# First MoE of a fused retention and MoE kernel: relu and square emitted right behind the first product, rounding ahead of the chunks' copies, the stream's second product in another bank

## The chip, the cores and the metric

The kernel runs on one core of one Trainium2 chip. The metric is the device time of one execution in microseconds (us). Lower is better. Besides the plain timed runs there is one execution under the hardware profiler, from which all rows below come.

## The reference

Three stages follow each other: a retention (linear attention with decay) over 4 batches, 8 heads, 768 positions and 64 features; a dense MoE over all 3072 tokens; and a second MoE with 8 experts, to which tokens are assigned greedily by their logits. The change is in the dense one.

```python
def _moe_ref(x, w_in, w_out, s, b):      # x 3072x512, w_in 512x2048, w_out 2048x512
    h = x @ w_in
    r = np.maximum(h, 0.0)
    g = s * (r * r) + b
    return (g @ w_out).astype(np.float32)

def _moe2_ref(x, w_gate, w1, w2):
    logits = x @ w_gate                  # then: greedy, 384 tokens for each of 8 experts
    for e in range(E):
        mask = assigned == e
        out[mask] = np.maximum(x[mask] @ w1[e], 0.0) @ w2[e]
```

## The kernel before

Matrices are fed to TensorE as two rounded parts, a high one and a low one (`xh` and `xl`, `h` and `l` of a weight, `rh` and `rl` of the squared activations), and a product is three matmuls: high by high, high by low, low by high. So each activation of the dense MoE has to be rounded (high part) and subtracted (low part) before it can be used.

The 3072 tokens are 24 chunks of 128. Chunks 0 to 5 go through a first stage, whose order of work a planner writes out. Chunks 6 to 19 go through **the stream**, the function `moe1`, with which the change deals. It has five blocks: four of three chunks and one of two. For each block it walks over the 16 slices of 128 of the 2048 hidden features. One step n is one block and one slice, 80 steps in all. Step n has two units of work:

- `hu(n)`: first `low_parts` of the step before (VectorE makes `rl` of step n-1, L466), then **the first product** (`h_unit`, L445): 12 matmuls of 384 columns (256 in the last block) into bank 3 of PSUM, always bank 3.
- `xu(n)`: **the second product** (`x_unit`, L477) of step n-2: nine matmuls of 512 columns (six in the last block) that are added to banks 0, 1 and 2, one bank a chunk. If this was the last slice of its block, the finished chunks are then copied out of their banks (`x_out`, L485, ScalarE). Then ScalarE works on step n: relu from bank 3 into the buffer `r` (L589, there is only one such buffer, `WR`), square in place (L458), and the rounding copy into `rh` (L459). `rh` and `rl` have two slots, by n modulo 2, so the rounding of step n overwrites what the second product of step n-2 reads.

So TensorE's order is: first product of n, second product of n-2, first product of n+1, second product of n-1, and so on. The first product of n+1 writes bank 3 and must wait until the relu of n has read it.

Between the units stand side streams (`Weave`): `attn`, which does the retention of the next chunks in steps (scale q on VectorE, L247; scores on TensorE, L352; mask, L357; values, state and cross products, L365, L373, L379; then ScalarE copies the chunk's result `xh`, L421 or L418, and the state `sbd`, L385, and VectorE makes `xl`, L422), and `logits_gen`, which lets VectorE multiply finished rows with the gate's columns (L497). A side step is due at a time counted along the stream, and is emitted ahead of the unit that is next when it comes due, so it may stand ahead of `hu(n)` or between `hu(n)` and `xu(n)`.

When the stream starts, the first stage has one second product of two chunks left (`REST`). It is emitted right behind `hu(0)`, with the copies of its two chunks. At steps 0 and 1 there is no second product yet, so the first products of steps 1 and 2 stand next to each other on TensorE.

After the stream come the last four chunks (`h_pair`), the search for the assignment, and the second MoE. Every engine works through its own instructions in the order in which they are emitted.

Of the kernel before, what the change touches and what calls it, by code (L numbers as in the profile page):

```python
# [27 lines left out]
AF = mybir.ActivationFunctionType  # L28
# [116 lines left out]
def kernel(  # L145
# [29 lines left out]
    NF = w64.shape[0]  # L175
# [16 lines left out]
    PE, ACT, DVE, POOL, SP = nc.tensor, nc.scalar, nc.vector, nc.gpsimd, nc.sync  # L192

    def bank(i):
        return psum.tile([128, 512], F32, name=f"b{i}", tag=f"b{i}")
# [23 lines left out]
    WR = work.tile([128, 2 * TB], F32, name="r")  # L219
# [219 lines left out]
    def h_part(f, ph, x, kcs):  # L439
        xh, xl = x  # L440
        wh, wl = WT[2 * f]
        for kc in kcs:
            ks = slice(kc * 128, (kc + 1) * 128)
            for n, (a, b) in enumerate(((wh, xh), (wh, xl), (wl, xh))):
                PE.matmul(ph, a[:, ks], b[..., kc, :], start=(kc == 0 and n == 0), stop=(kc == KC - 1 and n == 2))  # L445

    def h_unit(x, f, hb, n):

        ph = bank(hb)[:, 0:n]
        h_part(f, ph, x, range(KC))  # L450
        return ph
# [3 lines left out]
    def r_split(r, rh, rl):  # L455


        ACT.activation(r, r, AF.Square)  # L458
        ACT.activation(rh, r, AF.Copy)  # L459
        LOW.append((r, rh, rl))  # L460
        return rh, rl

    def low_parts():
        while LOW:
            r, rh, rl = LOW.pop(0)
            DVE.tensor_tensor(rl, r, rh.bitcast(F32), op=OP.subtract)  # L466

    def x_unit(chs, f, xb, r):

        rh, rl = r  # L470
        wh, wl = WT[2 * f + 1]
        for t, ch in enumerate(chs):
            if f == 0:
                X2[ch] = bank(xb[t])
            ts = slice(t * C, (t + 1) * C)
            for i, (a, b) in enumerate(((rh, wh), (rh, wl), (rl, wh))):
                PE.matmul(X2[ch], a[:, ts], b, start=(f == 0 and i == 0), stop=(f == NF - 1 and i == 2))  # L477
# [5 lines left out]
    def x_out(ch):  # L483
        U[ch] = tmp.tile([128, Dm], F32, name="tmp")
        ACT.activation(U[ch], X2[ch], AF.Copy, scale=sb[:, 0:1])  # L485
# [70 lines left out]
    def moe1(blocks, before):  # L556


        seq = [(i, f) for i in range(len(blocks)) for f in range(NF)]
        units, R = [], {}  # L560
        for n in range(len(seq) + 2):
            if n < len(seq):
                i, f = seq[n]
                chs = blocks[i]
                x = XS[(chs[0] - CPB) // 3 % 2] if len(chs) == 3 else [t[:, chs[0] // 2 % 2] for t in XP]

                def hu(n=n, i=i, f=f, x=x, w=len(chs) * C):
                    if f == 0:
                        before(i)
                    low_parts()  # L570
                    R[n] = h_unit(x, f, 3, w)
                units.append((len(chs) * 700, hu))

            def xu(n=n):
                if n == len(seq):
                    low_parts()
                    before(len(blocks))
                if n > 1:
                    i, f = seq[n - 2]
                    x_unit(blocks[i], f, range(3), R.pop(n - 2))  # L580
                    if f == NF - 1:
                        for ch in blocks[i]:
                            x_out(ch)
                if n < len(seq):

                    w = len(blocks[seq[n][0]]) * C
                    ws = slice(n % 2 * T3, n % 2 * T3 + w)
                    ph = R[n]
                    ACT.activation(WR[:, 0:w], ph, AF.Relu)  # L589
                    R[n] = r_split(WR[:, 0:w], RH[:, ws], RL[:, ws])  # L590
            units.append((len(blocks[seq[n - 2][0]]) * 695 if n > 1 else 0, xu))
        return units

# [213 lines left out]
    blocks = [range(ch, ch + 3) for ch in range(CPB, NC - 6, 3)] + [range(NC - 6, NC - 4)]  # L807
    nxt = []

    def before(i):  # L810

        while nxt and not nxt[0].done:
            nxt[0].step()
        if i < len(blocks):
            last = i + 1 == len(blocks)
            nxt[:] = [Side(attn(range(NC - 4, NC), (2800, 2500)) if last else attn(blocks[i + 1]),
                           wv.t + 6000 * (i == 0))]
            wv.add(nxt[0])
        else:
            split_last()  # L820

    for u in moe1(blocks, before):
        wv.unit(*u)
        if REST:
            wv.unit(1395, REST.pop())
            x_out(CPB - 2)
            x_out(CPB - 1)
# [52 lines left out]
    def h_pair(f):  # L880
        ph = bank(2 + f % 2)
        for i in range(2):
            wv.unit(1300, lambda: h_part(f, ph, XP, range(2 * i, 2 * i + 2)))
        r = r2[:, f % 2]
        ACT.activation(r, ph, AF.Relu)

        R4[f] = WT[2 * f]
        r_split(r, *R4[f])
        low_parts()

# [39 lines left out]
    for f in range(NF + 1):  # L930
        if f < NF:
            h_pair(f)
        if f == 1:
            wv.until(lambda: len(CONST) > NF)
            X2["l"] = bank(7)
        if f == NF:
            fill(4)
        if f >= 1:
            wv.unit(440, lambda: l_unit(f - 1))
# [642 lines left out]
```

## Time and profile before

| | |
|---|---|
| median of 3 runs | 995.09 us (994.17 to 997.15) |
| the profiled execution's own time | 993.34 us |
| span of its instructions | 991.6 us |
| TensorE busy | 965.8 us (97% of the span) |
| VectorE busy | 696.6 us (70%) |
| ScalarE busy | 445.5 us (45%) |
| mean granted TensorE clock | 0.993 |

The span runs from the first to the last instruction in the trace; the execution's own time is 1.7 us longer than it. Busy time counts an engine as busy while at least one of its instructions runs. The stream takes the stretch from about 181 to 557 us.

### The profile page before, as it was taken

The numbers are of one execution on the slowest core, as the hardware profiler recorded it, in microseconds if no ns is written. First come the engines' busy times: TensorE is split into PE (matmuls) and PEld (weight loads), VectorE is DVE, ScalarE is ACT, GpSimd is POOL, SyncE is SP. The second block draws the span as 40 slices with busy tenths as digits, with TensorE's granted clock in tenths as the row PEclk, the third lists the DMA queues.
The fourth block names the chain that finished last, engine by engine and source line by source line (L and its number), as shares of the span: only waits on it lengthen the run. The fifth ranks groups of instructions, "written<-read, shape, count | busy, mean of one in ns | idle before, by whom it ended". The sixth has DMA issues, their size and how long they took to land.

```text
span 991.6 us, 17302 instructions
## 1 busy us (share of the span) xinstructions
PE 965.8 (97%) x6721; PEld 837.0 (84%) x6721; DVE 696.6 (70%) x1677; ACT 445.5 (45%) x818; POOL 91.4 (9%) x153
## 2 busy tenths in 40 slices
PE   7899999999999999999999999999999999999997
PEld 6788888788888888888988877888888888888996
DVE  5899993687888977988465342578888877886310
ACT  6666665433343333343343454155455363455211
POOL 2000000000000000000000100032213042140111
PEclk8999999999999999999999999999999999999999
DMA  9234342422132022122023100063454373365100
GB/s 348 93 130 164 131 151 94 171 75 82 46 84 98 12 64 76 46 72 65 1 76 117 55 1 1 13 223 119 143 165 141 117 232 113 124 215 200 54 32 32
DMA packets 32946, 103.49 MB, mean 104 GB/s; under 512 B 4512, under 2 KB 4896, under 8 KB 32864
## 3 DMA queue, kind: packets, MB, share of 16 engines
q1 hardware_dynamic: 28080, 88.15, 27.0%
q0 software_dynamic: 3920, 12.89, 3.8%
q10 hardware_dynamic: 864, 1.35, 0.4%
q8 instruction: 52, 0.85, 0.3%
q14 instruction: 30, 0.25, 0.1%
HBM read 89.53 MB, written 12.85 MB: 103 GB/s over the span
## 4 chain that ended last, share of the span: by engine, by line
PE 88%; issue 4%; DMA 4%; ACT 2%; POOL 1%; DVE 1%; SPq 0%; POOLq 0%; ACTq 0%; DVEq 0%
PE b L445 27%; PE b L477 22%; PE b L1401 11%; PE b L1381 10%; PE b L910 5%; PE b L1060 3%; PE b L365 3%; PE b L352 3%; PE b L379 2%; DMA eraw<-in_w_dram 1%; PE b L1256 1%; PE b L373 1%; PE b L893 1%; POOL out_dram L1409 1%; DMA first1h<-in_qkv_dram 1%
## 5 line engine op out<-in xcount | busy, mean ns | idle before, releaser
L497 DVE SCALAR_TENSOR_TENSOR scr<-tmp,wg 128x512 bf16<-128x512 f32 x288 | 198.4, 689 | 8.4 <-ACT tmp L485 2.0
L477 PE MATMUL b<-h,rh 128*128 128x512 f32 x320 | 127.0, 397 | 0.6 <-ACT rh L741 0.6
L477 PE MATMUL b<-l,rh 128*128 128x512 f32 x320 | 125.9, 393 | 0.0
L477 PE MATMUL b<-h,rl 128*128 128x512 f32 x320 | 125.8, 393 | 0.0
L445 PE MATMUL b<-xh,h 128*128 128x512 f32 (+2 forms) x320 | 113.4, 355 | 4.8 <-ACT r L589 4.7
L445 PE MATMUL b<-xh,l 128*128 128x512 f32 (+2 forms) x320 | 111.2, 348 | 0.0
L445 PE MATMUL b<-xl,h 128*128 128x512 f32 (+2 forms) x320 | 111.2, 347 | 0.0
L1381 PE MATMUL b<-gh,h 128*128 128x384 f32 x256 | 89.7, 350 | 0.0
L1353 ACT ACTIVATE h<-eraw 128x1024 fp32r<-128x1024 f32 x64 | 67.2, 1057 | 42.6 <-DMA eraw<-in_w_dram 39.1
L1381 PE MATMUL b<-gh,l 128*128 128x384 f32 x256 | 86.2, 337 | 0.0
L1381 PE MATMUL b<-gl,h 128*128 128x384 f32 x256 | 86.0, 336 | 0.0
L589 ACT ACTIVATE r<-b 128x384 f32<-128x384 f32 (+1 forms) x80 | 37.6, 469 | 106.1 <-PE b L445 87.1
L1363 DVE TENSOR_TENSOR l<-eraw,h 128x1024 fp32r<-128x1024 f32 x64 | 77.9, 1227 | 8.8 <-ACT h L1353 8.4
L1389 DVE SCALAR_TENSOR_TENSOR hl<-b,hh 128x384 fp32r<-128x384 f32 x64 | 35.5, 555 | 61.5 <-ACT hh L1386 61.0
L1401 PE MATMUL b<-h,hh 128*128 128x512 f32 x192 | 78.0, 406 | 0.0
L1386 ACT ACTIVATE hh<-b 128x384 fp32r<-128x384 f32 x64 | 31.4, 490 | 103.0 <-PE b L1381 95.5
L1401 PE MATMUL b<-h,hl 128*128 128x512 f32 x192 | 75.6, 394 | 0.0
L1401 PE MATMUL b<-l,hh 128*128 128x512 f32 x192 | 75.4, 393 | 0.0
L445 PEld LDWEIGHTS b<-xh,h 128*128 128x128 f32 x320 | 60.5, 189 | 16.3 <-ACT r L589 8.3
L466 DVE TENSOR_TENSOR rl<-r,rh 128x384 fp32r<-128x384 f32 (+1 forms) x80 | 42.2, 528 | 44.8 <-ACT rh L459 44.5
L477 PEld LDWEIGHTS b<-h,rl 128*128 128x128 f32 x320 | 60.1, 188 | 13.5 <-DVE rl L743 0.4
L477 PEld LDWEIGHTS b<-h,rh 128*128 128x128 f32 x320 | 60.2, 188 | 12.0 <-ACT rh L741 0.8
(274 smaller groups left out, 1993.2 us busy)
## 6 DMA issues: line engine op xcount, KB each, us to landing
eraw<-in_w_dram SPq DMA_DIRECT2D x64, 512.0 KB, 4.3
q<-in_qkv_dram SPq DMA_DIRECT2D x36, 512.0 KB, 5.1
raw<-in_w_dram SPq DMA_DIRECT2D x32, 512.0 KB, 4.4
x2d<-tmp SPq DMA_DIRECT2D x21, 256.0 KB, 6.0
qdec<-in_dec_dram SPq DMA_DIRECT2D x17, 256.0 KB, 2.7
wg<-in_wgT_dram SPq DMA_DIRECT2D x4, 512.0 KB, 4.2
x2d<-tmp ACTq DMA_DIRECT2D x3, 256.0 KB, 2.3
first1h<-in_qkv_dram SPq DMA_DIRECT2D x1, 512.0 KB, 7.1
```

The source lines that it names most:

```text
L445: PE.matmul(ph, a[:, ks], b[..., kc, :], start=(kc == 0 and n == 0), stop=(kc == KC - 1 and n == 2))
L466: DVE.tensor_tensor(rl, r, rh.bitcast(F32), op=OP.subtract)
L477: PE.matmul(X2[ch], a[:, ts], b, start=(f == 0 and i == 0), stop=(f == NF - 1 and i == 2))
L497: DVE.scalar_tensor_tensor(scr, x, 1.0, WG[e], op0=OP.mult, op1=OP.mult, accum_out=of[:, e:e + 1])
L589: ACT.activation(WR[:, 0:w], ph, AF.Relu)
L910: PE.matmul(XB[c][:, ns], a[:, cs], b[:, ns], start=(f == 0 and i == 0), stop=(f == NF - 1 and i == 2), skip_group_check=True)
L1353: ACT.activation(hi, ERAW[n], AF.Copy)
L1363: DVE.tensor_tensor(lo, ERAW.pop(n), hi.bitcast(F32), op=OP.subtract)
L1381: PE.matmul(ph, a[:, ks], b[:, kc, :], start=(kc == 0 and n == 0), stop=(kc == KC - 1 and n == 2))
L1386: ACT.activation(hh, ph, AF.Relu)
L1389: DVE.scalar_tensor_tensor(hl, ph, 0.0, hh.bitcast(F32), op0=OP.max, op1=OP.subtract)
L1401: PE.matmul(Y[i, t], a[:, ts], b, start=(f == 0 and j == 0), stop=(f == NF2 - 1 and j == 2))
```

## The change

Three things are written differently.

1. Relu and square of step n are emitted in `hu(n)`, right behind the first product of n, and no longer in `xu(n)`.
2. In `xu(n)` the rounding copy comes ahead of the copies `x_out` of a finished block.
3. The first product of step 1 goes to bank 5 in place of bank 3.

`r_split` loses its square; `h_pair`, which calls it too, gets the square written out in the same place, so nothing moves there.

```diff
     def r_split(r, rh, rl):
-        ACT.activation(r, r, AF.Square)
         ACT.activation(rh, r, AF.Copy)
         LOW.append((r, rh, rl))
         return rh, rl
...
                     if f == 0:
                         before(i)
                     low_parts()
-                    R[n] = h_unit(x, f, 3, w)
+
+                    ph = h_unit(x, f, 5 if n == 1 else 3, w)
+                    ACT.activation(WR[:, 0:w], ph, AF.Relu)
+                    ACT.activation(WR[:, 0:w], WR[:, 0:w], AF.Square)
                 units.append((len(chs) * 700, hu))
...
                 if n > 1:
                     i, f = seq[n - 2]
                     x_unit(blocks[i], f, range(3), R.pop(n - 2))
-                    if f == NF - 1:
-                        for ch in blocks[i]:
-                            x_out(ch)
                 if n < len(seq):
 
                     w = len(blocks[seq[n][0]]) * C
                     ws = slice(n % 2 * T3, n % 2 * T3 + w)
-                    ph = R[n]
-                    ACT.activation(WR[:, 0:w], ph, AF.Relu)
                     R[n] = r_split(WR[:, 0:w], RH[:, ws], RL[:, ws])
+                if n > 1 and f == NF - 1:
+                    for ch in blocks[i]:
+                        x_out(ch)
...
         R4[f] = WT[2 * f]
+        ACT.activation(r, r, AF.Square)
         r_split(r, *R4[f])
         low_parts()
```

On VectorE, GpSimd and SyncE the order of instructions is the same as before. On TensorE it is the same too, but for the 12 matmuls of step 1, which write bank 5. What moves is on ScalarE, at three kinds of places. A name such as `b3_1676` is bank 3 in its use number 1676; a number in another name tells uses of a tile apart. In the changed kernel the relu is L572, the square L573, the rounding copy L458 and the copy of a finished chunk L484.

The start of the stream, before: `tmp` are the copies of the two chunks that the first stage has left, then follow steps 0, 1 and 2.

```order
L485 ACTIVATE tmp_1697<-b6_544,sb_73 128x512
L485 ACTIVATE tmp_1699<-b7_548,sb_73 128x512
L589 ACTIVATE r_90<-b3_1676 128x384
L458 ACTIVATE r_90<-r_90 128x384
L459 ACTIVATE rh_91<-r_90 128x384
L589 ACTIVATE r_90<-b3_1706 128x384
L458 ACTIVATE r_90<-r_90 128x384
L459 ACTIVATE rh_91<-r_90 128x384
L589 ACTIVATE r_90<-b3_1726 128x384
```

The same place after.

```order
L572 ACTIVATE r_90<-b3_1676 128x384
L573 ACTIVATE r_90<-r_90 128x384
L484 ACTIVATE tmp_1697<-b6_544,sb_73 128x512
L484 ACTIVATE tmp_1699<-b7_548,sb_73 128x512
L458 ACTIVATE rh_91<-r_90 128x384
L572 ACTIVATE r_90<-b5_1706 128x384
L573 ACTIVATE r_90<-r_90 128x384
L458 ACTIVATE rh_91<-r_90 128x384
L572 ACTIVATE r_90<-b3_1726 128x384
```

Relu and square of step 0 stand ahead of the two copies, its rounding behind them, and step 1 is read from bank 5.

The end of the first block of three chunks, before: the copies of banks 0, 1 and 2, the relu of the step whose first product is in bank 3, and behind it the copies `xh` and `sbd` of a retention step.

```order
L485 ACTIVATE tmp_2364<-b0_1744,sb_73 128x512
L485 ACTIVATE tmp_2366<-b1_1748,sb_73 128x512
L485 ACTIVATE tmp_2368<-b2_1752,sb_73 128x512
L589 ACTIVATE r_90<-b3_2337 128x384
L458 ACTIVATE r_90<-r_90 128x384
L459 ACTIVATE rh_91<-r_90 128x384
L421 ACTIVATE xh_100<-b5_2391 128x4x128
L385 ACTIVATE sbd_81<-b4_2323 64x4x64 x2
L589 ACTIVATE r_90<-b3_2376 128x384
L458 ACTIVATE r_90<-r_90 128x384
```

The same place after.

```order
L572 ACTIVATE r_90<-b3_2337 128x384
L573 ACTIVATE r_90<-r_90 128x384
L458 ACTIVATE rh_91<-r_90 128x384
L484 ACTIVATE tmp_2367<-b0_1746,sb_73 128x512
L484 ACTIVATE tmp_2369<-b1_1750,sb_73 128x512
L484 ACTIVATE tmp_2371<-b2_1754,sb_73 128x512
L572 ACTIVATE r_90<-b3_2376 128x384
L573 ACTIVATE r_90<-r_90 128x384
L421 ACTIVATE xh_100<-b5_2393 128x4x128
L385 ACTIVATE sbd_81<-b4_2323 64x4x64 x2
```

Relu, square and rounding of the step stand ahead of the block's three copies, and the next step's relu and square stand ahead of the retention step's copies.

A retention step in the last block, before: `tmp` is here the chunk's result, `sbd` the state.

```order
L418 ACTIVATE tmp_4546<-b5_4525 128x2x128
L418 ACTIVATE tmp_4547<-b5_4525 128x2x128
L385 ACTIVATE sbd_81<-b4_3595 64x4x64 x2
L589 ACTIVATE r_90<-b3_4511 128x256
L458 ACTIVATE r_90<-r_90 128x256
L459 ACTIVATE rh_91<-r_90 128x256
```

The same place after.

```order
L572 ACTIVATE r_90<-b3_4511 128x256
L573 ACTIVATE r_90<-r_90 128x256
L418 ACTIVATE tmp_4548<-b5_4527 128x2x128
L418 ACTIVATE tmp_4549<-b5_4527 128x2x128
L385 ACTIVATE sbd_81<-b4_3595 64x4x64 x2
L458 ACTIVATE rh_91<-r_90 128x256
```

Relu and square pass the retention step's copies, the rounding does not. This is so at nine of the stream's fifteen retention steps with such copies; at the other six the step stands ahead of `hu(n)`, and nothing moves.

## Rows read from the trace of the kernel before

**Rows 1.** Windows: stretch, busy us of each engine, granted clock, DMA share, GB/s.

```profile
264.00:274.00 10.00, 8.84 (x69) 7.61 (x69) 7.20 (x18) 4.88 (x10) 0.00 (x0) 1.00 0.02 3
...
180.00:557.00 377.00, 369.79 (x2416) 326.63 (x2415) 286.57 (x731) 144.04 (x297) 3.93 (x20) 1.00 0.23 70
```

**Rows 2.** Waits of TensorE, 180 to 560 us: total us, times, longest.

```profile
PE b L445 <- ACT r L589: 7.0, 8, 1.2
```

**Rows 3.** Timeline, TensorE, first block end: start, us, what, [idle before <- releaser].

```profile
267.36 0.40 PE L477 MATMUL b<-l,rh 128*128 128x512 f32 x1
267.59 0.40 PE L477 MATMUL b<-h,rl 128*128 128x512 f32 x1
269.14 0.45 PE L445 MATMUL b<-xht,h 128*128 128x384 f32 x1 [1.16 <-ACT r L589]
269.43 0.34 PE L445 MATMUL b<-xlt,h 128*128 128x384 f32 x1
269.60 0.34 PE L445 MATMUL b<-xht,l 128*128 128x384 f32 x1
```

**Rows 4.** Timeline, ScalarE, the same place.

```profile
266.63 2.08 ACT L485 ACTIVATE tmp<-b,sb 128x512 f32<-128x512 f32 x3 [3.73 <-PE b L477]
268.61 0.48 ACT L589 ACTIVATE r<-b 128x384 f32<-128x384 f32 x1
269.12 0.53 ACT L458 ACTIVATE r<-r 128x384 f32<-128x384 f32 x1
269.68 0.52 ACT L459 ACTIVATE rh<-r 128x384 fp32r<-128x384 f32 x1
```

**Rows 5.** Groups of instructions, ScalarE, 180 to 560 us: busy, mean ns, idle before.

```profile
L589 ACT ACTIVATE r<-b 128x384 f32<-128x384 f32 x64 | 31.4, 491 | 87.2 <-PE b L445 79.9 <-DVE rl L466 3.7 <-DVE scr L497 3.5
```

**Rows 6.** Timeline, TensorE, start of the stream.

```profile
182.51 0.33 PE L445 MATMUL b<-xh,l 128*128 128x384 f32 x1
...
183.84 0.40 PE L477 MATMUL b<-h,rl 128*128 128x512 f32 x1
185.39 0.44 PE L445 MATMUL b<-xh,h 128*128 128x384 f32 x1 [1.16 <-ACT r L589]
...
187.43 0.34 PE L445 MATMUL b<-xh,l 128*128 128x384 f32 x1
188.35 0.44 PE L445 MATMUL b<-xh,h 128*128 128x384 f32 x1 [0.58 <-ACT r L589]
...
192.72 1.16 PE L352 MATMUL b<-q 64*128 64x128 f32 x16
```

**Rows 7.** Timeline, ScalarE, start of the stream.

```profile
183.58 1.38 ACT L485 ACTIVATE tmp<-b,sb 128x512 f32<-128x512 f32 x2 [2.55 <-PE b L477]
```

**Rows 8.** Timeline, VectorE, start of the stream.

```profile
186.49 0.56 DVE L466 TENSOR_TENSOR rl<-r,rh 128x384 fp32r<-128x384 f32 x1 [2.07 <-ACT rh L459]
...
189.44 0.56 DVE L466 TENSOR_TENSOR rl<-r,rh 128x384 fp32r<-128x384 f32 x1 [0.32 <-ACT rh L459]
...
191.26 0.69 DVE L247 TENSOR_TENSOR q<-q,qdec 128x512 f32<-128x512 f32 x1
```

**Rows 9.** Timeline, TensorE, fourth block end and two retention steps.

```profile
503.36 0.39 PE L445 MATMUL b<-xh,h 128*128 128x256 f32 x1 [1.05 <-ACT r L589]
...
509.39 0.39 PE L445 MATMUL b<-xh,h 128*128 128x256 f32 x1 [0.36 <-ACT r L589]
...
538.03 0.39 PE L445 MATMUL b<-xh,h 128*128 128x256 f32 x1 [0.42 <-ACT r L589]
```

**Rows 10.** Timeline, TensorE and ScalarE, the last block.

```profile
513.62 0.28 PE L445 MATMUL b<-xh,l 128*128 128x256 f32 x1
...
515.36 0.39 ACT L589 ACTIVATE r<-b 128x256 f32<-128x256 f32 x1 [2.61 <-DVE rl L466]
...
516.41 0.28 PE L445 MATMUL b<-xh,h 128*128 128x256 f32 x1
```

**Rows 11.** Timeline, VectorE, the last block.

```profile
512.29 0.69 DVE L247 TENSOR_TENSOR q<-q,qdec 128x512 f32<-128x512 f32 x1 [0.26 <-DMA q<-in_qkv_dram]
```

## The prediction

> **What bounds the kernel now.** I read the windows first, then the waits of TensorE, then the timeline at each of those waits. In the stretch of the stream TensorE is busy 369.79 of 377 us and no other engine more than 286.57 [rows 1], so what is to be gained is the time in which TensorE stands still. The waits name one cause for all of it: eight times, 7.0 us in all, the first product (L445) waits for the relu (L589) [rows 2]. In the timeline of the first block end the reader is to see why. The second product's last matmul starts at 267.59, the next first product only at 269.14 [rows 3], because ScalarE copies three finished chunks (2.08 us from 266.63) before it comes to the relu at 268.61, although the relu's input has been ready since before the second product began [rows 4]. At a normal step the relu starts when its product ends: of the 87.2 us that ScalarE idles ahead of the 64 wide relus, 79.9 end with TensorE's L445 [rows 5]. It takes 0.49, and the second product that covers it is nine matmuls at a pitch of 0.23 (267.59 less 267.36 [rows 3]), 2.1 us. So in order the relu has some 1.6 us to spare, and TensorE stops only where ScalarE has something else ahead of it. The granted clock is 1.00 around that stall too [rows 1], so a stall costs its own length and no slow matmuls behind it.
>
> **What one stall costs.** The idle time in a row is too short by two pieces. A matmul's row is 0.40 long while the next one could start 0.23 after it, so 0.17 of standing still is hidden in the last row; and the first matmul behind a stall takes 0.29 until the second starts, against 0.17 from there on (269.43, 269.60 [rows 3]), another 0.1. The Trainium skill, Perfetto Trace Analysis, Identifying the Most-Contended Engine, says that busy time of matmuls is a bad measure since they are pipelined; summed by idle time, all eight waits are worth 7.0 us, and summed by starts they are worth 9.2 before anything else gets in the way.
>
> **The change part by part.**
>
> *Block ends, three chunks.* Three of them (269.14 and two more like it) have the same 1.16. From start to start: 267.59 + 0.23 = 267.82 could have been, 269.14 was, 1.32, and 0.1 for the refill: 1.42 each, 4.3 in all. With the change the relu comes behind its own product and nothing of ScalarE is ahead of it. What is late next are the copies out of banks 0 to 2. The rounding now stands ahead of them and must wait for the end of the second product, whose `rh` slot it overwrites. That end is 267.59 + 0.40 = 267.99; rounding 0.52 [rows 4] to about 268.55, then three copies of 0.69 each (2.08/3): 269.25, 269.95, 270.6. The next second product, which writes these banks anew, starts one first product later, 267.82 + 12 x 0.17 = 269.9, and takes bank after bank in steps of 0.7. Each copy is 0.65 ahead of its need, more where a retention step lies between. I cost this at nothing; without that cover it would be about 0.7 at each of four block ends, 2.8.
>
> *Block end, fourth.* Idle 1.05 [rows 9], plus 0.17 and 0.1: 1.3.
>
> *Retention steps.* At 509.39 and 538.03 the relu stands behind a chunk's result and state [rows 9]. Those go behind it: 0.36 + 0.27 and 0.42 + 0.27, 1.3 together. The copies of the result cannot be late by this as long as relu and square (0.49 + 0.53) are done before the cross product ends. Squares are neither added nor removed, and in `h_pair` nothing moves: nothing.
>
> *Start of the stream.* Two stalls stand here: 183.84 + 0.23 = 184.07 against 185.39, 1.32; and 187.43 + 0.17 = 187.60 against 188.35, 0.75 [rows 6]. With two refills 2.3. The first goes because relu 0 starts at 182.84, where its product ends, and not behind two copies at 183.58 [rows 7]. The second needs the other bank: the first products of steps 1 and 2 follow each other directly, and in bank 3 the second of them would still wait for the relu of step 1. But the gain does not all arrive. The scores (L352) would be ready to start at 192.72 - 2.3 = 190.4, and need the scaled q of VectorE, L247, which starts at 191.26 and takes 0.69 [rows 6, 8]. VectorE had waited 2.07 and 0.32 for the rounding of steps 0 and 1 [rows 8]. The rounding of step 0 now comes behind relu, square and two copies: 182.84 + 1.05 + 1.4 + 0.55 = 185.85, against 186.45 before, so VectorE is 0.6 earlier, and with the 0.32 gone 0.9. L247 then ends at 191.05, and TensorE stands still from 190.4 until there. What stays of the 2.3 is 192.72 - 191.05 less a refill, 1.6. So the other bank alone buys little, 0.2 to 0.3, since TensorE would wait for VectorE anyway.
>
> *The last block behind 510.* Here the relu waits for VectorE: at 515.36 until `rl` of the step before is made [rows 10], in a chain that starts at 512.29 with the landing of the chunk's q [rows 11]. That load is issued when the chunk before has been used, which is ahead of the stall at 509.39, so it does not come earlier by that stall's 0.63. The relu ends at 515.75, and the product that needs it starts at 516.41: slack 0.66, which takes up the 0.63 just so. I take nothing off; the other bound is that 0.6 is lost.
>
> *Sum.* 4.3 + 1.3 + 1.3 + 1.6 = 8.5; I round down to 8.4 for the last point. The profiled execution took 993.34 (span 991.6), so 984.9. The median is 1.75 above that execution, at 995.09, and what I forecast is the like of the median: 986.7. Behind 557 us nothing is changed, and everything there hangs on the stream's results, so I take the gain to arrive whole.
>
> **The rivals.**
>
> *Half of it, as VectorE takes over.* VectorE is busy 286.57 of 377 [rows 1] and follows its own order, which is unchanged. Its gate products may now wait for the later copies of the chunks, hold back the `rl` behind them and so the next relu, 0.7 at each of four block ends; with the 0.6 of the last block the gain is 8.4 - 2.8 - 0.6 = 5, and the time 990. For it speaks that VectorE did set the pace behind 512 [rows 10]; against it that only 3.7 of 87.2 us ahead of the wide relus were waits for `rl` [rows 5].
>
> *The waits stay, the change does not do what it says.* The relu could be held by something other than ScalarE's order: it writes the one buffer `r`, which VectorE must have read for `rl` of the step before. If that is so at the block ends, only the start's 1.6 is won: 993.5. Against it: at 268.61 the relu follows the copies with no idle time [rows 4]. The Trainium skill, Perfetto Trace Analysis, Matmuls, says that independent groups of matmuls should rotate through banks so that reading one overlaps the next group; 79 of 80 first products stay in bank 3, so by that rule alone the block ends would still stall. No price of mine rests on it, for the steps in between already run in one bank without a stall.
>
> *Slower.* In nine retention steps the chunk's result now stands behind a relu that may wait for `rl`. ScalarE is held, `xl` on VectorE behind it, and the next `rl` behind that. Where the relu is later than its product's end by more than the retention step's products last, each of the nine loses the excess. At 515.36 it is 1.46 late (513.62 + 0.28 [rows 10]); were all nine to lose 1.3, that is 11.7 against 8.4 won: 998.4. It decides from 0.9 a step on. Against it stand the 3.7 us over 64 relus [rows 5].
>
> **How the numbers follow.** The forecast has 0.77, its own range 985 to 988.5 (the start's losses undone or the last block's 0.6 lost, and the spread of the runs, whose median can lie a us off). Half has 0.12, the waits stay 0.06, slower 0.05. The range reaches from 984.0 to 991.5: it leaves out the last two and the edges of the rest. Within 0.3%, about 3 us, is what a measurement of this kernel cannot tell from no change; the forecast and half lie beyond it, so faster 0.89, same 0.06, slower 0.05.
>
> **What would show it.** In the profile after: the eight waits of L445 for the relu gone or below 0.3 in total; at the block ends the relu right behind its product and the three copies behind the rounding; the next second product without a wait for them; at the start a wait of TensorE's scores for VectorE of about half a us; span near 983. It would be wrong if the first product waits for the relu as before, if L477 waits for the chunks' copies, or if VectorE's idle time ahead of L497 grows at the block ends and the relus wait for `rl`; or if the stream ends 8 us earlier and the routing behind it gives that back.

## The result and the profile after

The changed kernel takes 986.47 us (median of 6 runs, 986.07 to 987.37), beside 995.22 us for the kernel before on the same chip (6 runs). The ratio is 0.9914, 95% interval 0.9901 to 0.9926: 8.75 us less. The forecast was 986.7, in the range 984.0 to 991.5.

The profiled execution took 986.66 us, its span is 984.7. That span is only 6.9 shorter than the one before, so the stages have to be looked at one by one. These are windows of the kernel before: the stream, from the start of its first 384-column matmul to the start of the last matmul of its last second product; the stretch up to the first gather of the second MoE; and the rest.

```profile
180.58:560.94 380.36, 373.15 (x2430) 329.44 (x2429) 288.38 (x738) 146.27 (x302) 3.93 (x20) 1.00 0.23 70
560.94:656.50 95.56, 95.56 (x586) 74.16 (x585) 45.74 (x143) 41.78 (x67) 3.14 (x9) 1.00 0.11 37
656.50:991.60 335.10, 326.32 (x2550) 287.74 (x2548) 226.13 (x631) 142.29 (x221) 78.66 (x116) 0.99 0.41 133
```

The same three stretches of the changed kernel.

```profile
181.24:552.77 371.53, 371.17 (x2430) 330.48 (x2429) 287.92 (x738) 145.22 (x302) 3.88 (x20) 1.00 0.24 72
552.77:648.34 95.57, 95.57 (x586) 74.16 (x585) 45.74 (x143) 41.84 (x67) 3.13 (x9) 1.00 0.11 37
648.34:984.70 336.36, 326.71 (x2550) 287.83 (x2548) 225.66 (x631) 142.05 (x221) 77.72 (x116) 0.99 0.40 133
```

The stream is 8.83 us shorter, and TensorE now stands still in it for 0.36 us by its busy time, against 7.21. The next stretch is the same to 0.01. The last one is 1.3 longer and the time ahead of the stream 0.7; neither is touched by the change, and over the ten other profiled executions of this study the last stretch takes anything from 334.9 to 336.4. So the stream's length, which differed by 0.12 between two executions of the changed kernel (371.53 here, 371.41 in the second), is the better yardstick for parts of the change, and the times are the check on it.

The waits of TensorE between 178 and 560 us in the changed kernel, which answer to [rows 2]. The first lies ahead of the stream and was there before.

```profile
PE b L445 <- ACT scr L737: 0.5, 1, 0.5
PE b L352 <- DVE q L247: 0.2, 1, 0.2
```

All eight waits for the relu are gone. One new one has come, at the scores, where it was forecast, but 0.2 long and not half a us. The first block end on TensorE, for [rows 3]:

```profile
265.94 0.40 PE L476 MATMUL b<-l,rh 128*128 128x512 f32 x1
266.18 0.39 PE L476 MATMUL b<-h,rl 128*128 128x512 f32 x1
266.41 0.33 PE L445 MATMUL b<-xht,h 128*128 128x384 f32 x1
266.58 0.34 PE L445 MATMUL b<-xlt,h 128*128 128x384 f32 x1
...
270.10 0.50 PE L476 MATMUL b<-h,rh 128*128 128x512 f32 x1
```

And on ScalarE, for [rows 4]:

```profile
264.52 0.49 ACT L572 ACTIVATE r<-b 128x384 f32<-128x384 f32 x1 [3.02 <-PE b L445]
265.05 0.53 ACT L573 ACTIVATE r<-r 128x384 f32<-128x384 f32 x1
266.44 0.53 ACT L458 ACTIVATE rh<-r 128x384 fp32r<-128x384 f32 x1 [0.86 <-PE b L476]
266.87 1.83 ACT L484 ACTIVATE tmp<-b,sb 128x512 f32<-128x512 f32 x3
268.72 0.49 ACT L572 ACTIVATE r<-b 128x384 f32<-128x384 f32 x1
```

Here the next first product (266.41) follows the last matmul of the second product (266.18) at that product's pitch of 0.23, with no wait between. The relu starts at 264.52, when its product ends, the rounding comes behind it, then the three copies. They are done at 268.70, and the second product that needs their banks starts at 270.10.

### The profile page after: what moved, and what is told of

Read it like the earlier page. It is cut to its first block, busy times and chain, and to the rows that moved or that the text cites. A ratio compares the mean times of both kernels' runs of the same rounds, so it can differ in the third digit from the quotient of the medians.

```text
span 984.7 us, 17311 instructions
## 1 busy us (share of the span) xinstructions
PE 964.3 (98%) x6721; PEld 838.2 (85%) x6721; DVE 696.4 (71%) x1677; ACT 444.3 (45%) x818; POOL 90.4 (9%) x153
## 4 chain that ended last, share of the span: by engine, by line
PE 86%; issue 4%; DMA 4%; DVE 2%; POOL 2%; ACT 1%; SPq 0%; POOLq 0%; DVEq 0%; ACTq 0%
PE b L445 26%; PE b L476 22%; PE b L1402 10%; PE b L1382 10%; PE b L911 5%; PE b L365 3%; PE b L1061 2%; PE b L352 2%; PE b L379 2%; DMA big<-x2d,idx 1%; PE b L1257 1%; PE b L373 1%; PE b L894 1%; DMA eraw<-in_w_dram 1%; POOL out_dram L1410 1%
## 5 line engine op out<-in xcount | busy, mean ns | idle before, releaser
L572 ACT ACTIVATE r<-b 128x384 f32<-128x384 f32 (+1 forms) x80 | 37.6, 470 | 134.1 <-PE b L445 111.4
L458 ACT ACTIVATE rh<-r 128x384 fp32r<-128x384 f32 (+1 forms) x80 | 40.3, 504 | 67.3 <-PE b L476 67.1
L476 PEld LDWEIGHTS b<-l,rh 128*128 128x128 f32 x320 | 60.2, 188 | 10.0
```

## The experiments

All but two are the changed kernel as it is or with one part undone or moved; r_halves adds something to it, and bank_alone is the kernel before with one part of the change. The length of the stream is taken from the trace of each, the times are medians with the kernel before on the same chip beside them.

| run | time | before, same chip | ratio, 95% interval | stream |
|---|---|---|---|---|
| again | 985.55 | 993.62 | 0.9907 (0.9888 to 0.9926) | 371.41 |
| ends_back | 991.47 | 993.62 | 0.9972 (0.9959 to 0.9986) | 377.26 |
| steps_back | 985.64 | 993.62 | 0.9905 (0.9885 to 0.9925) | 372.77 |
| start_back | 988.14 | 993.62 | 0.9933 (0.9912 to 0.9954) | 373.71 |
| bank_back | 985.89 | 994.67 | 0.9909 (0.9891 to 0.9927) | 372.18 |
| bank_alone | 993.77 | 994.67 | 0.9992 (0.9978 to 1.0006) | 379.13 |
| copies_first | 985.50 | 994.67 | 0.9910 (0.9891 to 0.9930) | 371.59 |
| r_halves | 986.21 | 994.67 | 0.9916 (0.9898 to 0.9933) | 371.05 |
| copies_later | 985.97 | 995.45 | 0.9907 (0.9893 to 0.9920) | 371.69 |

**again**: the changed kernel once more.

> The changed kernel once more, as the yardstick of this chip. Theory (the gain is the sum of the removed stalls of TensorE, start to start: block ends 5.6, retention steps 1.3, start of the stream 1.6): about 986.5 us, 8.5 under the kernel before, and in the trace the stretch from the stream's first 384-column matmul to its last second product near 371.5 us, against 380.4 before. Rival (the gain sits in the other bank, or in VectorE getting its input earlier): the same here; the three kernels beside it tell them apart.

The stream is 371.41; I take the mean of both executions, 371.47, as the yardstick below.

**ends_back**: the order at the four block ends undone.

```diff
-                    ph = h_unit(x, f, 5 if n == 1 else 3, w)
-                    ACT.activation(WR[:, 0:w], ph, AF.Relu)
-                    ACT.activation(WR[:, 0:w], WR[:, 0:w], AF.Square)
+                    ph = R[n] = h_unit(x, f, 5 if n == 1 else 3, w)
+                    if n < 2 or seq[n - 2][1] < NF - 1:
+                        ACT.activation(WR[:, 0:w], ph, AF.Relu)
+                        ACT.activation(WR[:, 0:w], WR[:, 0:w], AF.Square)
...
+                if n > 1 and f == NF - 1:
+                    for ch in blocks[i]:
+                        x_out(ch)
                 if n < len(seq):
...
+                    if n > 1 and f == NF - 1:
+                        ACT.activation(WR[:, 0:w], R[n], AF.Relu)
+                        ACT.activation(WR[:, 0:w], WR[:, 0:w], AF.Square)
                     R[n] = r_split(WR[:, 0:w], RH[:, ws], RL[:, ws])
-                if n > 1 and f == NF - 1:
-                    for ch in blocks[i]:
-                        x_out(ch)
```

> The changed kernel, but at the four block ends the chunks' copies stand again ahead of relu, square and rounding; start and retention steps stay as changed. Theory: the four stalls come back, 3 x 1.42 + 1.3 = 5.6, so stream near 377.1 and time near 992.1; four waits of the first product for the relu of about 1.1 each in the trace. Rival, other bank: nothing comes back, 986.5. Rival, VectorE paces: less than half comes back, under 989.3, with relus waiting for rl in place of it.

The stream grew by 5.79 and the time by 5.9 beside the changed kernel on the same chip. The waits of TensorE in its trace:

```profile
PE b L445 <- ACT r L592: 4.5, 4, 1.2
PE b L445 <- ACT r L573: 0.4, 1, 0.4
PE b L352 <- DVE q L247: 0.2, 1, 0.2
```

L592 is the relu that stands behind the copies: the four waits are back, and with them two thirds of the gain. Both rivals named there are out. The 0.4 is a wait in the last block for a relu that itself waits for `rl`; before and in the changed kernel it is 0.1, so some of the 5.79 is not the block ends' own. Behind the fourth block end the stream is 5.55 longer than the changed kernel's (180.05 to 505.89, against 181.24 to 501.53), which is the size of the four stalls.

**steps_back**: relu and square behind the retention steps' copies again, from step 2 on.

```diff
-                    ph = h_unit(x, f, 5 if n == 1 else 3, w)
-                    ACT.activation(WR[:, 0:w], ph, AF.Relu)
-                    ACT.activation(WR[:, 0:w], WR[:, 0:w], AF.Square)
+                    ph = R[n] = h_unit(x, f, 5 if n == 1 else 3, w)
+                    if n < 2:
+                        ACT.activation(WR[:, 0:w], ph, AF.Relu)
+                        ACT.activation(WR[:, 0:w], WR[:, 0:w], AF.Square)
...
                     ws = slice(n % 2 * T3, n % 2 * T3 + w)
+                    if n > 1:
+                        ACT.activation(WR[:, 0:w], R[n], AF.Relu)
+                        ACT.activation(WR[:, 0:w], WR[:, 0:w], AF.Square)
                     R[n] = r_split(WR[:, 0:w], RH[:, ws], RL[:, ws])
```

> The changed kernel, but from step 2 on relu and square are emitted at the head of the second product's unit again, so that a retention step's copies come ahead of them; still ahead of the chunks' copies. Theory: only the two stalls at retention steps of the last block come back, 0.63 and 0.69, so stream near 372.8 and time near 987.8. Rival (it is the early relu throughout that pays): 3 or more comes back, 989.5 or more. Rival, other bank: 986.5.

The stream grew by 1.30, with two waits for the relu:

```profile
PE b L445 <- ACT r L589: 0.8, 2, 0.4
PE b L352 <- DVE q L247: 0.2, 1, 0.2
```

The time does not show it (985.64 against 985.55): its runs lie between 983.9 and 987.0, which is wider than what is sought. The trace decides for the theory: the two stalls stand at the two places named, and start to start with the refill each is worth what was expected, 0.63 and 0.69. That the time bears it out is not shown. That the whole stream grew by just 1.30 is partly chance, for about 0.2 came on in small delays in the blocks before and about 0.2 was taken up in the last block.

**start_back**: steps 0 and 1 as before.

```diff
-                    ph = h_unit(x, f, 5 if n == 1 else 3, w)
-                    ACT.activation(WR[:, 0:w], ph, AF.Relu)
-                    ACT.activation(WR[:, 0:w], WR[:, 0:w], AF.Square)
+                    ph = R[n] = h_unit(x, f, 3, w)
+                    if n > 1:
+                        ACT.activation(WR[:, 0:w], ph, AF.Relu)
+                        ACT.activation(WR[:, 0:w], WR[:, 0:w], AF.Square)
...
                     ws = slice(n % 2 * T3, n % 2 * T3 + w)
+                    if n < 2:
+                        ACT.activation(WR[:, 0:w], R[n], AF.Relu)
+                        ACT.activation(WR[:, 0:w], WR[:, 0:w], AF.Square)
                     R[n] = r_split(WR[:, 0:w], RH[:, ws], RL[:, ws])
```

> The changed kernel, but steps 0 and 1 as before: relu 0 behind the two copies of the first stage, first product of step 1 in bank 3. Theory: 1.6 comes back, stream near 373.1 and time near 988.1, with the two waits of 1.2 and 0.6 in the trace and no wait of the scores for the scaled q. Rival, other bank: most of the 8.5 comes back, above 990.

```profile
PE b L445 <- ACT r L589: 1.7, 2, 1.2
PE b L352 <- issue: 0.2, 1, 0.2
```

The two waits are back, 1.2 and 0.6, and the wait of the scores at the start is gone; the one shown lies at 521.7. But the stream grew by 2.24 (time: 2.6), and not by 1.6. The part was there, its size was not right. The stream's first matmul and the last one of the first block:

```profile
180.58 0.33 PE L445 MATMUL b<-xh,h 128*128 128x384 f32 x1
...
267.57 0.39 PE L476 MATMUL b<-h,rl 128*128 128x512 f32 x1
```

They lie 86.99 apart, against 84.94 in the changed kernel (181.24 to 266.18): 2.05 of the 2.24 came back right at the start, and most of the rest much later, in the last block.

**bank_back**: only the other bank undone, that of the first product of step 1. (The title's "second product" is this one, the second that the stream makes, and not `x_unit`.)

```diff
-                    ph = h_unit(x, f, 5 if n == 1 else 3, w)
+                    ph = h_unit(x, f, 3, w)
```

> The changed kernel, but the first product of step 1 in bank 3 as before; the order on ScalarE stays as changed. Theory: its product of step 2 waits for the relu of step 1 again (idle 0.6, with tail and refill 0.85), but TensorE would wait at the scores for VectorE in any case, so only 0.2 to 0.3 comes back: stream 371.7 to 371.8, time within 0.3 of the changed kernel, and the wait of the scores for q is gone. Rival (the other bank carries the gain of the start): 0.85 or more comes back in the stream.

```profile
PE b L445 <- ACT r L572: 0.6, 1, 0.6
```

The wait is the expected one, and the scores wait no more. The stream grew by 0.71, three times what I gave the bank and nearer to the 0.85 that I had left to the rival. The time cannot tell (985.89 beside copies_first's 985.50).

**bank_alone**: the kernel before with only the other bank.

```diff
-                    R[n] = h_unit(x, f, 3, w)
+                    R[n] = h_unit(x, f, 5 if n == 1 else 3, w)
```

> The kernel before, and of the change only the other bank for the first product of step 1. Theory: of the two stalls at the start the second goes, 0.85, but the scores can come only 0.77 earlier before they wait for the scaled q of VectorE (start 192.72 against its end 191.95), so stream 380.4 - 0.75 = 379.6 and time 0.75 under before, which the times can hardly tell; the same edit that is worth 0.25 on top of the rest is worth three times that alone. Rival (bank 3 is what binds at the block ends too): more than 2 us.

```profile
PE b L445 <- ACT r L589: 5.3, 6, 1.2
PE b L352 <- DVE q L247: 1.1, 1, 1.1
```

The stream is 1.2 shorter than before, where I had expected 0.75. Of the eight waits not one but two are gone. I had read the bank wrongly here: the first stall of the start is the first product of step 1 waiting for bank 3 as well, and in bank 5 it waits for nothing. So either edit takes the first stall away, and the second needs the bank. Both stalls together are 2.3, of which VectorE then takes 1.1 at the scores, because relu, square and rounding of step 0 are still behind the copies. The time, 0.9992 (0.9978 to 1.0006), is the same as before.

**copies_first**: at a block end the copies ahead of the rounding again, relu and square early.

```diff
+                if n > 1 and f == NF - 1:
+                    for ch in blocks[i]:
+                        x_out(ch)
                 if n < len(seq):
...
                     R[n] = r_split(WR[:, 0:w], RH[:, ws], RL[:, ws])
-                if n > 1 and f == NF - 1:
-                    for ch in blocks[i]:
-                        x_out(ch)
```

> The changed kernel, but at the block ends the chunks' copies come ahead of the rounding again; relu and square stay ahead of both. Theory: the rounding is needed only two units later, so nothing comes back: stream 371.3 to 371.8, time within 0.3 of the changed kernel; the copies start up to 1.5 us earlier, the rounding about 0.8 later. Rival (rounding ahead of the copies is what frees VectorE, so that rl and the next relu are in time): 1 us or more comes back, with relus waiting for rl behind the block ends.

The stream is 371.59, 0.1 from the yardstick. The second part of the change, rounding ahead of the copies, is worth nothing that these traces can tell; at the block ends the early relu does it.

**copies_later**: the copies put off once more, behind the next step's relu and square.

```diff
                     ACT.activation(WR[:, 0:w], WR[:, 0:w], AF.Square)
+                    if n > 2 and seq[n - 3][1] == NF - 1:
+                        for ch in blocks[seq[n - 3][0]]:
+                            x_out(ch)
...
-                if n > 1 and f == NF - 1:
+                if n == len(seq) + 1:
                     for ch in blocks[i]:
                         x_out(ch)
```

> The changed kernel, but the chunks' copies of a block end are put off by one more step, behind relu and square of the next step. It doubles the delay that I costed at nothing. Theory: the copies then start when the next first product has been read and squared, about 1.05 after that product's end, while the next block's second product wants bank 0 right there, or 1.7 to 2.9 later where a retention step stands between. So of the four block ends those with only values and state between (the first and the third) should show TensorE's second product waiting 0.3 to 0.6 for a chunk's copy, with refill 0.4 to 0.7 each, the other two nothing: stream 0.8 to 1.5 longer, 372.3 to 373, time near 987.5. Rival (the copies have much more cover than 0.65 us): no wait, 986.5. Rival (they have none to spare): 2.8 or more.

The waits are where they were expected, at the first and the third block end, and of the expected kind. The waits of TensorE, and ScalarE at the first of the two:

```profile
PE b L476 <- ACT tmp L484: 0.4, 2, 0.2
PE b L352 <- DVE q L247: 0.2, 1, 0.2
```

```profile
269.31 0.52 ACT L573 ACTIVATE r<-r 128x384 f32<-128x384 f32 x1
269.74 1.83 ACT L484 ACTIVATE tmp<-b,sb 128x512 f32<-128x512 f32 x3
271.45 0.61 ACT L421 ACTIVATE xh<-b 128x512 fp32r<-128x512 f32 x1
```

But each wait is 0.2, or 0.3 with the refill, where 0.4 to 0.7 was expected. Three copies took 1.83 where I had counted 2.08, and the first starts 0.1 before the square ends. Behind the fourth block end the stream is 0.58 late (181.32 to 502.19, against 181.24 to 501.53 in the changed kernel), yet in the end it is only 0.2 longer: the last block took up the rest. The sign was right and the size too large, and the stream's length alone makes it look smaller than it was.

**r_halves**: the changed kernel, and in the last block the relu writes its buffer's halves in turn.

```diff
+        def rbuf(n, w):
+            o = n % 2 * w if w <= TB else 0
+            return WR[:, o:o + w]
...
-                    ACT.activation(WR[:, 0:w], ph, AF.Relu)
-                    ACT.activation(WR[:, 0:w], WR[:, 0:w], AF.Square)
+                    ACT.activation(rbuf(n, w), ph, AF.Relu)
+                    ACT.activation(rbuf(n, w), rbuf(n, w), AF.Square)
...
-                    R[n] = r_split(WR[:, 0:w], RH[:, ws], RL[:, ws])
+                    R[n] = r_split(rbuf(n, w), RH[:, ws], RL[:, ws])
```

> The changed kernel, and in the last block, where a step is 256 columns wide, the relu writes the two halves of its buffer in turn, so that it no longer waits for VectorE to have read the step before. Theory: TensorE is held by that wait in two places only, about 0.25 and 0.1, so the stream gets 0.2 to 0.4 shorter, 371.1 to 371.3, and the time is the same within its noise; the waits of the relu for rl (over 11 us of ScalarE's idle time in the last block) go. Rival (the one buffer is what paces the last block, and TensorE was kept by it in more than it shows): 1 us or more off.

Waits of ScalarE in its stream (L576 is the relu), and of the changed kernel's (L572):

```profile
ACT r L576 <- DVE rl L465: 0.8, 1, 0.8
```

```profile
ACT r L572 <- DVE rl L465: 16.3, 9, 3.3
```

Of 16.3 us of such waits 0.8 are left, and the stream is 0.42 shorter, 371.05, the shortest here, in one execution. The time, 986.21, does not differ from the other runs of the changed kernel: in the trace this version is ahead of it, in the times it only ties.

## Why the prediction was right

**What bounds, and what a stall costs.** Right. The stream lost 8.83 us, where idle time alone gave 7.0 [rows 2]; the tail hidden in the last matmul's row and the refill are the difference, and the experiments that bring single stalls back bring them back at that size: 5.55 for four block ends, 1.3 for two retention steps. One reading was off: at the first block end the relu's input was ready not before the second product began (265.74) but 0.15 after it (265.56 + 0.33). That leaves 0.7 us until the copies begin, and nothing changes by it.

**Block ends.** 5.6 forecast, 5.55 came back at the block ends in ends_back. **Retention steps.** 1.3 forecast, 1.3 came back. **The rounding ahead of the copies at nothing**: copies_first shows it, 0.1. The rounding did not have to wait for the end of the second product, as was said: its last matmul reads `rl`, and the rounding started 0.10 after the end of the last one that reads `rh` (265.94 + 0.40, 266.44).

**Start of the stream.** Here is the term that was mis-sized: 1.6 forecast, 2.05 came back at this place in start_back, and 2.07 is what the change itself won there (180.58 to 267.59 before, 181.24 to 266.18 after). The mechanism was as said: both stalls go, 2.3, and the scores then wait for the scaled q. But they wait 0.2 and not 0.6. This is ScalarE and VectorE in the changed kernel at that place, for [rows 7, 8]:

```profile
183.54 0.49 ACT L572 ACTIVATE r<-b 128x384 f32<-128x384 f32 x1 [1.85 <-PE b L445]
184.07 0.53 ACT L573 ACTIVATE r<-r 128x384 f32<-128x384 f32 x1
184.50 1.25 ACT L484 ACTIVATE tmp<-b,sb 128x512 f32<-128x512 f32 x2
185.64 0.52 ACT L458 ACTIVATE rh<-r 128x384 fp32r<-128x384 f32 x1
```

```profile
186.19 0.56 DVE L465 TENSOR_TENSOR rl<-r,rh 128x384 fp32r<-128x384 f32 x1 [1.10 <-ACT rh L458]
...
190.56 0.69 DVE L247 TENSOR_TENSOR q<-q,qdec 128x512 f32<-128x512 f32 x1
```

From relu to the end of the rounding I had put 3.0; it took 2.62 (183.54 to 186.16). I took 1.4 for two copies from [rows 7] and 2.08 for three from [rows 4]. Those are not the copies' own pace: there each copy waited for its chunk's matmuls, which end 0.7 apart. Where the input is ready, the first of two copies starts 0.10 before the square ends, the pair takes 1.25, and the rounding starts 0.11 before it ends. The Trainium skill, ScalarE: Activation LUTs, What ACT_TABLE_LOAD costs, says that back-to-back ACTIVATEs overlap by about 93 ns; the trace agrees for instructions that do not depend on each other (0.10 and 0.11 here), and not for a square behind its own relu (184.03 to 184.07, no overlap). So VectorE came 0.4 sooner, and the other bank was worth 0.6 to 0.7 on top of the rest and not 0.2 to 0.3. The same pace gives the copies more cover at the block ends than the 0.65 I had counted, which is one reason why copies_later cost so little.

**The last block.** Right in the mechanism, and 0.1 too small. This is the place of [rows 10, 11] in the changed kernel, on VectorE, ScalarE and TensorE:

```profile
505.30 0.69 DVE L247 TENSOR_TENSOR q<-q,qdec 128x512 f32<-128x512 f32 x1 [1.11 <-DMA q<-in_qkv_dram]
```

```profile
508.37 0.39 ACT L572 ACTIVATE r<-b 128x256 f32<-128x256 f32 x1 [3.33 <-DVE rl L465]
```

```profile
508.46 0.40 PE L476 MATMUL b<-h,rl 128*128 128x512 f32 x1
508.80 0.38 PE L445 MATMUL b<-xh,h 128*128 128x256 f32 x1
509.02 0.28 PE L445 MATMUL b<-xl,h 128*128 128x256 f32 x1
```

Counted from the stream's start, L247 comes 7.65 earlier than before (324.06 against 331.71), while TensorE is 8.4 ahead when the retention step's stall is gone: the load of q did not come earlier by that stall. The slack took up most of the 0.63, and 0.2 was lost: the first product starts 0.34 after the matmul ahead of it in place of 0.23, and its second matmul 0.22 later in place of 0.12. The forecast had allowed 0.1. r_halves, where the relu no longer waits for `rl`, gives 0.42 back, here and at two places behind it; that is what the one buffer `r` cost.

**The rivals.** The half: VectorE did wait longer for the copies, on the page its idle time ahead of the gate products rose from 8.4 to 9.2, 2.9 of it for `tmp` where it had been 2.0, but no relu of a wide step held TensorE up by it. The waits stay: out, by the waits of the changed kernel. In particular 79 of 80 first products still use bank 3, and none of them shows an idle wait of more than 0.1, so the bank was not what bound the block ends. Slower: the relu does wait for `rl` in the last block, 15.5 us of idle time ahead of it, but the chunks' results were not late by it: in all fifteen retention steps the copy of the result starts 0.04 to 0.05 after the product that it reads has ended.

**The sum.** Undone one by one, the parts lengthen the stream by 5.79 + 1.30 + 2.24 = 9.3, and together it gained 8.9 by the yardstick. The difference lies in the last block, whose waits shift with everything ahead of it: counted where the parts stand, they are 5.55 + 1.3 + 2.05 = 8.9. Forecast were 8.4. The time came out 0.2 from the forecast, closer than its terms were, and that is partly luck: the start was put 0.45 too low, and the changed kernel's own median was 986.47 in one measurement and 985.55 in the other. The span was 984.7 and not near 983, since what lies outside the stream took 1.9 longer in that execution.

## What to carry to other kernels

On an engine that works in order, put the instruction that frees the busiest engine's buffer right behind its producer, and let the copies that are needed later wait; here that was nearly all of the gain. The second bank, for one product, brought 0.6 to 0.7 of it, and a second buffer gave 0.4 more, in the trace alone. When you price a sequence from a trace, ask of every repeated row whether it ran at its own pace or at that of what it waited for: three copies in 2.08 us were TensorE's pace, and took 1.83 when nothing held them. Judge a part that is smaller than the spread of the times by its own stretch of the trace.

## What was not expected of the hardware

A slot of `rh` came free before the second product had ended. At the block end above, the last matmul that reads `rh` (265.94) has a row that ends at 266.34, and the product's last matmul, which reads `rl`, one that ends at 266.57. The rounding, which overwrites `rh`, starts at 266.44, between the two (the ends of matmul rows are modelled). It waited for the last reader of its own slot and not for the product's end.

At the start of the stream before, TensorE stood still for 1.32 and 0.75 us within 4.3 us, and the granted clock of the whole stream is 1.00, the 2.4 GHz level, before and after.
